# A fused attention and gated-MLP kernel: the second batch's first head pair goes through the opening, transposed by TensorE

## The chip, the cores and the metric

The kernel runs on one core of a Trainium2 chip. A core has five engines that run side by side, each with its own stream of instructions: TensorE (PE in the profile; its weight loads are listed apart as PEld), VectorE (DVE), ScalarE (ACT), GpSimd (POOL) and SyncE (SP), which here only issues DMA transfers. They meet at semaphores. PE writes into PSUM, which has eight banks here: four singles (the tags m0 to m3) and two doubles (s0, s1). Everything else lies in SBUF, 128 partitions wide.

The metric is the device time of one execution in microseconds (us); lower is better.

## The reference, cut to what matters

```
# q, k, v: (8 batches, 8 heads, 576 positions, 64)
scores = q @ k.T / 8
scores = where(block_i >= block_j, scores, -1e9)    # blocks of 64 positions
attn = exp(scores - max); attn = attn / (sum(attn) + 1e-9)
x = (attn @ v), heads side by side                  # (8, 576, 512)
h = relu(x @ w_in)                                  # 1024 wide
u, v = h[..., :512], h[..., 512:]
v_n = (v - mean(v)) / sqrt(var(v) + 1e-6)
v_s = w_spatial @ v_n + b_spatial                   # over the 576 positions
out = (u * v_s) @ w_out
```

## The kernel before

Work is counted in **pairs** of heads (four to a batch, 32 in all) and in **batches** of the MLP (eight). The batches' MLP matmuls are "M" work; they use a split of each number in a high and a low part and three products in place of one. A batch of M consists of five groups of v (L1103; the fifth is short, for the last 64 positions), eight groups of u (L1213), eight spatial groups (L1250 to L1257) and eight output groups (L1302). `moe(b, ready)` lists them; the string `order` says in which order the groups of v and u come. All groups of v of a batch need x, the attention's result, of all four pairs of that batch.

There are two forms of attention.

- **The opening** (function `opening`) does the four pairs of batch 0, cut into 16 units (k, pair): `unit(k, pr)` takes query rows in four parts k = 0 to 3. For each unit: scores on PE (L897, L907), row maxima on DVE with a mask added (L935, L941), exponentials on ACT (L951), sums on POOL and their reciprocal on DVE, a scaling on POOL or ACT (L370, L372), then PE transposes the scaled scores in blocks of 128 x 128 (L993) into PSUM, ACT or DVE copies them into the tile pt (L366), and PE multiplies them with v (L1021). The result is split into x by ACT (L1036) and DVE (L1040). Scaled scores of all units lie in the two buffers of the tile p, at places that `place(k, pr)` gives; a place is used again when the transposes that read it are through. Parts of pt serve in turn, three of them.
- **All later pairs** (function `attention`) do their scores in one row of instructions (L587, L603), the softmax on the same engines (L657, L663, L685, L698, L704, L372), and then DVE transposes blocks of 32 x 32 inside each partition group (L726) and 16 transfers of SyncE's queue regroup the blocks from p into pt (L734). There is one tile pt, and a pair's regroup waits until the products of the pair before it (L750) are through. There are two buffers of p. For the keys to come out in the right order, the host permutes k for these pairs. Batch 1 (`plain`) takes q and k as they are, later batches split them into a high and a low part (`need`).

**The order of all instructions is fixed ahead**, by the class `Line`: every piece of work is added with its engine, an assumed duration, what it comes after, which buffers it takes and drops (`Hold`, `Ring`, `Banks`) and a rank; `play` then goes through time and gives each engine the ready piece of the lowest rank. PE has four lanes, in each of which the order is kept: S (scores), T (transposes), A (products), M (the MLP). `pick_pe` takes A, T or S ahead of M when they are ready; a piece's `slack` is added to the time at which it counts as ready; a `gate` holds a score or a product back until a given amount of M work has been spent (`LEAD`, `MATE`, `MATE_LEAD`). Where the plan has a long wait on PE, `bridge` fills it with `pad` matmuls (L346, L350), which compute nothing. SyncE's queue is ordered by rank in the same way: loads of raw q and k, of v and of weights, the regroup, and the stores of the output.

**Weights** are prepared in the same stretch: w_in (L426 to L446, L393, L396), in two halves (for v and for u), w_spatial and w_out, each loaded into one of two staging tiles, converted on DVE, ACT and POOL and split. The last argument of `prep_w_in`, `prep_w_sp`, `prep_w_tail` and `prep_w_out` is the rank.

**Tiles that serve twice**: the mask of the opening (`mask0`) lies in the tile vl3, which the first MLP batch needs later; v_n waits for it by `mask_hold`. `tails[b]` (tag xs, two buffers) holds the last 64 positions of x of a batch.

Of the kernel before, what the change touches and what calls it, by code (L numbers as in the profile page):

```python
# [17 lines left out]
P = 128  # L18
S = 576
# [238 lines left out]
def kernel(  # L258
# [41 lines left out]
    mask0 = ff_p.tile([P, S], F32, tag="vl3", name="mask0")  # L300
# [60 lines left out]
    mask_hold = given(r_vn, 9 * NPAIR + 14)  # L361
# [39 lines left out]
    def prep_w(hi, lo, w, rows, cols, name, rank):  # L401
# [10 lines left out]
        f_hold = mask_hold if home else Hold(r_vr, 2)  # L412
# [102 lines left out]
    def attention(b, pr):  # L515
# [213 lines left out]
        for j in range(4):  # L729
            for i in range(4):  # L730
                def regroup(i=i, j=j):
                    if "pt" not in box:
                        box["pt"] = pt_p.tile([P, 4, NT, 32], F32, tag="pt", name=f"pt_{nm}")
                    nc.sync.dma_start(  # L734
                        box["pt"][32 * j:32 * j + 32, i], box["pp"][32 * i:32 * i + 32, j]
                    )
# [39 lines left out]
        al.slack = 100 if plain else None  # L776
# [34 lines left out]
    def opening():  # L811

        boxes = [{} for _ in range(NPAIR)]
# [26 lines left out]

        def load_part(pr, n):
            spans = (slice(0, 256), slice(Q0, Q0 + 256)), (slice(256, Q0), slice(Q0 + 256, KQ))
            for m, cs in enumerate(spans[n]):
                def fn(cs=cs, start=n == m == 0):
                    if start:
                        boxes[pr]["raw"] = raw_tile(pr)
                    nc.sync.dma_start(boxes[pr]["raw"][:, cs], qk[0, pr, :, cs])
# [3 lines left out]
                    "SP", 340, fn, takes=takes,  # L851
                    rank=-4 + 0.01 * len(got), size=P * 4 * (cs.stop - cs.start)))

        def load_v(pr):
            def fn():
                if pr < 2:
# [5 lines left out]
                nc.sync.dma_start(t, v[0, pr])  # L862
# [12 lines left out]
        load_v(3)  # L875

        def unit(k, pr):
            nm = f"0_{pr}_{k}"
# [49 lines left out]
            for r, (hd, o, n, at) in enumerate(runs):  # L928
# [36 lines left out]
            a = add("POOL", 190, guard, after=sums, rank=-1)  # L965
            a = add("DVE", 165, lambda: nc.vector.reciprocal(box["sum"][:, 4:4 + n], box["sum"][:, 0:n]),
                    after=[a], rank=-1.5)
            muls = [[], []]
            for r, (hd, _, cols, _) in enumerate(runs):
# [3 lines left out]
                m = add(("POOL", "ACT"), (240 + 0.825 * cols, 120 + 0.845 * cols), scale, after=[a], rank=0)  # L973
# [5 lines left out]
            for z, (t0, m) in enumerate(split):  # L979
# [15 lines left out]
                def move(eng, z=z, t0=t0, m=m):  # L995
# [8 lines left out]
                                 after=[a], drops=[t_hold], rank=-0.5))  # L1004
# [26 lines left out]
            def high():  # L1031
                if k == 0:
                    xts[0, pr] = xt_p.tile([P, 2, S], F32R, tag="x", name=f"x_0_{pr}")
                    if pr == 0:
                        tails[0] = ff_p.tile([P, NPAIR, 2, 64], F32R, tag="xs", name="xs_0", bufs=2)
                nc.scalar.copy(xts[0, pr][:, 0, q0:q0 + n_q], box["av"][:, 0, :n_q])  # L1036
# [7 lines left out]

            takes = [x_hold[0, pr]] + ([xs_hold[0]] if pr == 0 else []) if k == 0 else []
            h = add("ACT", 60 + 0.82 * n_q, high, after=[a], takes=takes, drops=[a_hold], rank=-3,
                    behind=x_done.get((0, pr), [])[:1])
            x_done.setdefault((0, pr), []).append(
                add("DVE", 70 + 1.045 * n_q, low, after=[h], drops=[a_hold], rank=-3))
            if k == 3:  # L1050
                def tail():
                    nc.gpsimd.tensor_scalar(
                        out=tails[0][:, pr], in0=xts[0, pr][:, :, FULL * P:].bitcast(F32), scalar1=1.0,
# [3 lines left out]
                xs_done[0, pr] = add("POOL", 271, tail, after=x_done[0, pr], rank=-1)  # L1057

        for k in range(4):
            for pr in range(NPAIR):  # L1060
                unit(k, pr)

    def x_need(b, first, last):

        edges = (256, 384, 512, 576) if b == 0 else (256, 576)
        return [
            x_done[b, pr][n] for pr in range(NPAIR) for n, (lo, hi) in enumerate(zip((0, *edges), edges))
# [5 lines left out]
    def moe(b, ready):  # L1073
# [164 lines left out]
        def sp_group(z, dc):  # L1238
# [35 lines left out]
            def rest():  # L1274
# [10 lines left out]
                    wide=True, rank=0.2 if last else 0.6)  # L1285
# [41 lines left out]
        order = "vuvuvuvuvuuuu" if b else "vvvvuuuuuvuuu"  # L1327
# [87 lines left out]
```

## Time and profile before

| | us |
|---|---|
| median of 3 runs | 673.7 (673.68 to 673.82) |
| the profiled execution | 671.56 |
| its span, first to last instruction | 669.8 |
| granted TensorE clock, mean | 1.00 |

A line of the timeline has the start, the length, the engine, the line of the kernel, the operation with what it writes and reads, the shape and the count; idle time ahead of it and what ended that stand in brackets. A matmul's length overlaps the next one's, so the price of one in a row is the distance between starts. SPq is SyncE's DMA queue. A line of the windows has a stretch and its length, then for PE, PEld, DVE, ACT and POOL the busy time and the number of instructions, then the granted clock, the mean share of the DMA engines and GB/s. A line of the groups has an engine, an operation, its count, the busy time, the mean ns of one, and the idle time before them with what ended most of it.

### The profile page before, as it was taken

The page shows a single profiled execution, that of the slowest core. Times are in us where ns is not written, and L with a number is a line of the kernel's source. Part 1 is how long each engine was busy: PE and PEld are TensorE (multiplying, and loading weights), DVE is VectorE, ACT ScalarE, POOL GpSimd, SP SyncE. Part 2 cuts the span into 40 slices and gives each one's busy share as a digit, 9 for nine tenths or more (in the row PEclk, how much of TensorE's full clock was granted, in tenths as well). Part 3 has the DMA queues.
Part 4 walks back from the last instruction along what each step waited for, and adds up shares of the span by engine and source line. Part 5 has one row for each costly group of instructions (what it writes and reads, how often), then busy time and mean ns, then how long its engine had stood idle before and what let it go on. Part 6 is the DMA issues. An engine that isn't in the chain of part 4 may idle for free.

```text
span 669.8 us, 15587 instructions
## 1 busy us (share of the span) xinstructions
PE 656.6 (98%) x5430; PEld 583.2 (87%) x5430; DVE 492.6 (74%) x1382; ACT 376.2 (56%) x1059; POOL 353.2 (53%) x688
## 2 busy tenths in 40 slices
PE   8999989989999999999999999999999999999998
PEld 5587978878999888998899888999889988999997
DVE  6989899766887669866898568877698668823522
ACT  7879777445755566545765645556665446512320
POOL 5377754365566635655656447665456556511111
PEclk9999999999999999999999999999999999999999
DMA  8164566664566664566456665585645664451002
GB/s 284 48 203 153 157 168 188 175 170 120 158 157 178 174 158 126 148 173 175 119 146 145 168 169 129 118 213 152 164 118 140 176 166 109 120 129 42 1 1 71
DMA packets 44210, 95.57 MB, mean 143 GB/s; under 512 B 9698, under 2 KB 19938, under 8 KB 44132
## 3 DMA queue, kind: packets, MB, share of 16 engines
q1 hardware_dynamic: 44132, 94.58, 52.6%
q8 instruction: 43, 0.70, 0.5%
q14 instruction: 35, 0.29, 0.1%
HBM read 39.23 MB, written 9.44 MB: 73 GB/s over the span
## 4 chain that ended last, share of the span: by engine, by line
PE 87%; SPq 5%; ACT 3%; DVE 2%; DMA 2%; issue 1%; POOL 1%; POOLq 0%; ACTq 0%
PE mo L1302 14%; PE mv L1103 14%; PE ms L1250 14%; PE mu L1213 12%; PE av L750 12%; PE s L587 8%; SPq L734 5%; PE s L603 3%; PE t L993 2%; PE av L1021 2%; ACT p L951 1%; PE ms L1255 1%; PE pad L350 1%; PE ms L1257 1%; PE s L907 1%
## 5 line engine op out<-in xcount | busy, mean ns | idle before, releaser
L372 POOL TENSOR_SCALAR p<-p,ssum 128x128 f32<-128x128 f32 (+5 forms) x261 | 152.2, 596 | 20.4 <-DVE ssum L704 8.8
L685 ACT ACTIVATE p<-p,nmax 128x128 f32<-128x128 f32 (+4 forms) x252 | 145.9, 581 | 26.1 <-DVE nmax L657 24.7
L726 DVE STREAM_TRANSPOSE p<-p 128x384 f32<-128x384 f32 (+2 forms) x196 | 121.3, 638 | 20.4 <-POOL p L372 19.2
L1213 PE MATMUL mu<-x,wi_hi 128*128 128x288 f32 x512 | 109.6, 295 | 0.0
L657 DVE CUSTOM_DVE_ANT_1 p<-s,mask 128x128 f32<-128x128 f32 (+1 forms) x224 | 95.3, 485 | 2.5 <-PE s L587 2.3
L750 PE MATMUL av<-pt,v 128*64 128x64 f32 (+2 forms) x1232 | 83.7, 291 | 6.7 <-DMA pt<-p 3.9
L750 PEld LDWEIGHTS av<-pt,v 128*64 128x64 f32 x1232 | 63.9, 137 | 28.5 <-issue 5.8
L1103 PE MATMUL mv<-wi_hi,x 128*128 128x512 f32 x256 | 87.1, 398 | 0.0
L1213 PEld LDWEIGHTS mu<-x,wi_hi 128*128 128x128 f32 x512 | 84.5, 188 | 1.8 <-DVE nmax L657 0.8
L1250 PE MATMUL ms<-ws_lo,vh 128*128 128x288 f32 x256 | 76.2, 298 | 0.0
L1250 PE MATMUL ms<-ws_hi,vh 128*128 128x288 f32 x256 | 75.8, 296 | 0.0
L1302 PE MATMUL mo<-gl,wo_hi 128*128 128x288 f32 x256 | 75.6, 295 | 0.0
L1250 PE MATMUL ms<-ws_hi,vl 128*128 128x288 f32 x256 | 75.6, 295 | 0.0
L1302 PE MATMUL mo<-gh,wo_lo 128*128 128x288 f32 x256 | 75.6, 295 | 0.0
L698 POOL TENSOR_SCALAR ssum<-ssum 128x4 f32<-128x4 f32 (+1 forms) x112 | 27.3, 243 | 91.2 <-ACT p L685 74.8
L1302 PE MATMUL mo<-gh,wo_hi 128*128 128x288 f32 x256 | 75.3, 294 | 0.0
L1213 PE MATMUL mu<-x,wi_lo 128*128 128x288 f32 x256 | 70.7, 297 | 0.0
L1272 ACT CAST gh<-u 128x288 fp32r<-128x288 f32 x64 | 25.9, 431 | 73.9 <-DVE u L1264 38.2
L790 DVE TENSOR_TENSOR x<-av,x 128x256 fp32r<-128x256 f32 (+1 forms) x56 | 25.4, 454 | 50.6 <-ACT x L787 50.2
L787 ACT CAST x<-av 128x256 fp32r<-128x256 f32 (+1 forms) x56 | 22.4, 399 | 69.2 <-PE av L750 69.1
L557 POOL TENSOR_TENSOR lo<-raw,hi 128x320 fp32r<-128x320 f32 (+1 forms) x72 | 57.7, 815 | 2.7 <-ACT hi L551 2.4
L1103 PEld LDWEIGHTS mv<-wi_hi,x 128*128 128x128 f32 x256 | 47.8, 188 | 12.6 <-issue 2.9
(130 smaller groups left out, 1541.9 us busy)
## 6 DMA issues: line engine op xcount, KB each, us to landing
pt<-p SPq DMA_DIRECT2D x448, 100.0 KB, 2.2
raw<-qk SPq DMA_DIRECT2D x28, 640.0 KB, 4.6
v<-v SPq DMA_DIRECT2D x32, 320.0 KB, 3.5
outT<-o SPq DMA_DIRECT2D x64, 144.0 KB, 2.0
rwi<-w_in SPq DMA_DIRECT2D x8, 512.0 KB, 4.6
rwo<-w_out SPq DMA_DIRECT2D x4, 512.0 KB, 3.9
raw<-qk SPq DMA_DIRECT2D x8, 192.0 KB, 4.7
rws<-w_spT SPq DMA_DIRECT2D x4, 288.0 KB, 3.2
```

The costliest lines, as they stand in the source:

```text
L372: nc.gpsimd.tensor_scalar(out=x, in0=x, scalar1=by, scalar2=1.0, op0=ALU.mult, op1=ALU.mult)
L557: eng.tensor_tensor(out=box["lo"][:, cs], in0=box["raw"][:, cs], in1=box["hi"][:, cs].bitcast(F32), op=ALU.subtract,)
L587: nc.tensor.matmul(by_block(bk[hd][:, o:o + n]), a[js, qs], keys(kk, js, n), start=(m == 0), stop=(m == len(parts) - 1),)
L657: nc.vector.tensor_tensor_reduce(out=out, in0=by_block(bk[hd][:, o:o + n]), in1=tiles(mask, 5 - t, t + 1), scale=-0.125, scalar=BIG, op0=A ...
L685: nc.scalar.activation(out, out, AF.Exp, bias=mx, scale=-1.0, accum_out=box["sum", k][:, c:c + 1],)
L726: nc.vector.transpose(x, x)
L734: nc.sync.dma_start(box["pt"][32 * j:32 * j + 32, i], box["pp"][32 * i:32 * i + 32, j])
L750: nc.tensor.matmul(box["av", z][js, q0:q1], box["v"][:, c, js], move(j), start=(n == 0), stop=(n == len(todo) - 1), skip_group_check=True,)
L1103: nc.tensor.matmul(box["ps"], a, w[:, k, DH:], start=(n == 0), stop=(n == len(todo) - 1))
L1213: nc.tensor.matmul(box["ps"][:, :HT], w[:, k, ds], xts[b, k][:, j, zs], start=(n == 0), stop=(n == len(todo) - 1),)
L1250: nc.tensor.matmul(box["ps"][:, :HT], vn[k][a][:, ds], w[:, k, zs], start=(n == 0), stop=False)
L1302: nc.tensor.matmul(box[ec, "ps"][:, :HT], w[:, k, es], a[:, k, :], start=(k == 0 and n == 0), stop=(last and n == 2),)
```

## The change

- Pair 0 of batch 1 (`MORE = 1`) leaves `attention` and becomes a fifth pair of `opening`: 4 more units, k = 0 to 3, put behind the 16 others, at four places of the second buffer of p. Its keys are not permuted by the host any more. Its ranks are by `LATER = 3` higher (less urgent) than those of batch 0. Its q and k come in four transfers into the tile raw when pair 0 of batch 0 is done with it.
- The mask's tile becomes a buffer of the tag xs, 512 wide, and is released after the row maxima of all 20 units; v_n waits for the weight preparation alone, and the second use of the other xs buffer (`tails[1]`, with the first x of the moved pair) waits for the mask.
- `LEAD` goes from 6.0 to 5.0: the gates of the pairs up to 9 (two pairs into batch 2) come a quarter batch of M work later.
- The regroup's rank goes from 2 to 1, the slack of batch 1's products from 100 to 1000 ns, the rank of w_in's u half from 0.7 to 0.65, of w_spatial from 1.45 to 0.8, of w_out from 2.6 to 1.1, and that of the gated low part on POOL from 0.6 to 0.3.
- The orders of the groups change: "vuvuvuvuvuuuu" becomes "vvuvuvuvuuuuu", and for batch 0 "vvvvuuuuuvuuu" becomes "vvvvuvuuuuuuu".

```diff
-LEAD = 6.0
+LEAD = 5.0
+MORE, LATER = 1, 3
...
-    mask0 = ff_p.tile([P, S], F32, tag="vl3", name="mask0")
+    mask0 = ff_p.tile([P, 512], F32, tag="xs", name="mask0", bufs=2)
...
-    mask_hold = given(r_vn, 9 * NPAIR + 14)
+    mask_hold, spare_hold = given(r_xs, 9 * (NPAIR + MORE)), given(r_vn, 14)
...
-                moved.append(add("SP", 635, regroup, after=done, drops=[pp_hold], rank=2, size=102400,
+                moved.append(add("SP", 635, regroup, after=done, drops=[pp_hold], rank=1, size=102400,
...
-        al.slack = 100 if plain else None
+        al.slack = 1000 if plain else None
...
-        boxes = [{} for _ in range(NPAIR)]
+        pairs = [(0, pr) for pr in range(NPAIR)] + [(1, pr) for pr in range(MORE)]
+        boxes = [{} for _ in pairs]
...
-        pp_holds = [Hold(r_pp, 7), Hold(r_pp, 9)]
+        pp_holds = [Hold(r_pp, 7), Hold(r_pp, 9 + 4 * MORE)]
...
+            if pr >= NPAIR:
+                return 1, (0, 3, 6, 10)[k], (3, 3, 4, 2)[k]
...
-        pt_hold = Hold(r_pt, 4 * NPAIR)
+        pt_hold = Hold(r_pt, 4 * len(pairs))
...
+        for pr in range(NPAIR, len(pairs)):
+            load_part(pr, 0)
+            load_part(pr, 1)
+            load_v(pr)
...
+            later = LATER if b else 0
...
-                a = add("DVE", 76 + 1.045 * n, rows, after=[op], drops=[s_hold[hd], mask_hold], rank=-2)
-                sums.append(add("ACT", 282 + 0.845 * n, exps, after=[a], rank=-1))
+                a = add("DVE", 76 + 1.045 * n, rows, after=[op], drops=[s_hold[hd], mask_hold], rank=later - 2)
+                sums.append(add("ACT", 282 + 0.845 * n, exps, after=[a], rank=later - 1))
...
+        for pr in range(NPAIR, len(pairs)):
+            for k in range(4):
+                unit(k, pr)
...
-                    wide=True, rank=0.2 if last else 0.6)
+                    wide=True, rank=0.2 if last else 0.3)
...
-        order = "vuvuvuvuvuuuu" if b else "vvvvuuuuuvuuu"
+        order = "vvuvuvuvuuuuu" if b else "vvvvuvuuuuuuu"
...
-    ready["u"] = [x for c in range(NC) for x in prep_w_in(c, 0, 0.7)]
-    ready["s"] = [x for c in range(FULL) for x in prep_w_sp(c, 1.45)] + prep_w_tail(1.45)
-    ready["o"] = [x for c in range(ND) for x in prep_w_out(c, 2.6)]
+    ready["u"] = [x for c in range(NC) for x in prep_w_in(c, 0, 0.65)]
+    ready["s"] = [x for c in range(FULL) for x in prep_w_sp(c, 0.8)] + prep_w_tail(0.8)
+    ready["o"] = [x for c in range(ND) for x in prep_w_out(c, 1.1)]
...
-        for pr in range(NPAIR):
+        for pr in range(MORE if b == 1 else 0, NPAIR):
             attention(b, pr)
...
+    qk[1, :MORE, :, :S], qk[1, :MORE, :, S:Q0] = kt[1, :MORE], 0
```

More of the change, by code (lines that the diff above doesn't have):

```diff
@@ L846, in fn @@
                         boxes[pr]["raw"] = raw_tile(pr)
-                    nc.sync.dma_start(boxes[pr]["raw"][:, cs], qk[0, pr, :, cs])
+                    nc.sync.dma_start(boxes[pr]["raw"][:, cs], qk[(*pairs[pr], slice(None), cs)])
                 takes = [raw_holds[pr]] if n == m == 0 else []
                 got.setdefault((pr, n), []).append(add(
-                    "SP", 340, fn, takes=takes,
+                    "SP", 340, fn, takes=takes, behind=() if takes else got[pr, 0][:1],
                     rank=-4 + 0.01 * len(got), size=P * 4 * (cs.stop - cs.start)))
@@ L855, in fn @@
             def fn():
-                if pr < 2:
+                if pr not in (2, 3):
                     t = v_p.tile([P, FULL + 1, P], F32, tag="v", name=f"v_0_{pr}")
@@ L963, in guard @@
                 )
-            a = add("POOL", 190, guard, after=sums, rank=-1)
+            a = add("POOL", 190, guard, after=sums, rank=later - 1)
             a = add("DVE", 165, lambda: nc.vector.reciprocal(box["sum"][:, 4:4 + n], box["sum"][:, 0:n]),
-                    after=[a], rank=-1.5)
+                    after=[a], rank=later - 1.5)
             muls = [[], []]
@@ L971, in scale @@
                     times(eng, box["run", r][0], box["sum"][:, 4 + r:5 + r])
-                m = add(("POOL", "ACT"), (240 + 0.825 * cols, 120 + 0.845 * cols), scale, after=[a], rank=0)
+                m = add(("POOL", "ACT"), (240 + 0.825 * cols, 120 + 0.845 * cols), scale, after=[a], rank=later)
                 muls[hd].append(m)
@@ L1003, in unit @@
                 moves.append(add(("ACT", "DVE"), (60 + 0.82 * P * m, 70 + 1.05 * P * m), move,
-                                 after=[a], drops=[t_hold], rank=-0.5))
+                                 after=[a], drops=[t_hold], rank=later - 0.5))
             q0, n_q = ((0, 256), (256, P), (384, P), (512, 64))[k]
@@ L1032, in high @@
                 if k == 0:
[L1033 to L1036, printed above, removed]
+                    xts[who] = xt_p.tile([P, 2, S], F32R, tag="x", name=f"x_{b}_{lane_pr}")
+                    if lane_pr == 0:
+                        tails[b] = ff_p.tile([P, NPAIR, 2, 64], F32R, tag="xs", name=f"xs_{b}", bufs=2)
+                nc.scalar.copy(xts[who][:, 0, q0:q0 + n_q], box["av"][:, 0, :n_q])
             def low():
-                x = xts[0, pr]
+                x = xts[who]
                 nc.vector.tensor_tensor(
@@ L1043, in low @@
                 )
[L1045 to L1049, printed above, removed]
+            takes = [x_hold[who]] + ([xs_hold[b]] if lane_pr == 0 else []) if k == 0 else []
+            h = add("ACT", 60 + 0.82 * n_q, high, after=[a], takes=takes, drops=[a_hold], rank=later - 3,
+                    behind=x_done.get(who, [])[:1])
+            x_done.setdefault(who, []).append(
+                add("DVE", 70 + 1.045 * n_q, low, after=[h], drops=[a_hold], rank=later - 3))
             if k == 3:
@@ L1052, in tail @@
                     nc.gpsimd.tensor_scalar(
-                        out=tails[0][:, pr], in0=xts[0, pr][:, :, FULL * P:].bitcast(F32), scalar1=1.0,
+                        out=tails[b][:, lane_pr], in0=xts[who][:, :, FULL * P:].bitcast(F32), scalar1=1.0,
                         scalar2=1.0, op0=ALU.mult, op1=ALU.mult,
                     )
-                xs_done[0, pr] = add("POOL", 271, tail, after=x_done[0, pr], rank=-1)
+                xs_done[who] = add("POOL", 271, tail, after=x_done[who], rank=later - 1)
         for k in range(4):
@@ L1061, in opening @@
                 unit(k, pr)
+        for pr in range(NPAIR, len(pairs)):
+            for k in range(4):
+                unit(k, pr)
     def x_need(b, first, last):
[L1065 removed]
+        edges = {4: (256, 384, 512, 576), 2: (256, 576)}
         return [
[L1067 removed]
+            done for pr in range(NPAIR) for x in [x_done[b, pr]]
+            for done, lo, hi in zip(x, (0, *edges[len(x)]), edges[len(x)])
             if lo < last and hi > first
```

13 lines of the change are left out of this document (7 added, 6 removed).

## The prediction, made before the changed kernel ran

> Pairs are called by batch and pair: 1.0 is the first pair of the second batch, the one that is moved. "Its products" are its score matrix times v (L750, and L1021 in the opening).
>
> **What bounds the kernel now.** The first look goes to the busy times and to the chain of work that ended last.
>
> ```profile
> span 669.8 us, 15587 instructions
> PE 656.6 (98%) x5430; PEld 583.2 (87%) x5430; DVE 492.6 (74%) x1382; ACT 376.2 (56%) x1059; POOL 353.2 (53%) x688
> PE 87%; SPq 5%; ACT 3%; DVE 2%; DMA 2%; issue 1%; POOL 1%; POOLq 0%; ACTq 0%
> ```
>
> TensorE (PE) is the bound of the whole; what can be won is 13.2 us of idle time (669.8 - 656.6) and whatever of the busy time is no work. The second look is at stretches cut at the places where pairs 1.0 to 1.3 get their products (columns: stretch, its length, busy time and count of PE, PEld, DVE, ACT, POOL, clock, DMA share, GB/s).
>
> ```profile
> 48.70:72.20 23.50, 23.50 (x148) 17.76 (x147) 22.60 (x74) 22.02 (x65) 17.68 (x32) 1.00 0.47 155
> 72.20:88.00 15.80, 13.31 (x95) 12.69 (x93) 13.30 (x26) 10.13 (x20) 9.03 (x12) 1.00 0.66 167
> 88.00:104.00 16.00, 14.68 (x130) 12.72 (x132) 15.80 (x44) 11.01 (x30) 7.72 (x15) 1.00 0.64 171
> 104.00:120.00 16.00, 15.01 (x129) 13.01 (x129) 14.53 (x44) 11.80 (x30) 6.55 (x13) 1.00 0.69 189
> 120.00:137.20 17.20, 15.53 (x145) 14.30 (x143) 10.76 (x33) 9.77 (x29) 9.25 (x16) 1.00 0.67 184
> 218.00:669.80 451.80, 448.46 (x3714) 407.69 (x3712) 311.78 (x855) 226.76 (x642) 227.85 (x451) 1.00 0.51 131
> ```
>
> From 218 us on PE is busy for 448.46 of 451.80 us; nothing that happens there can win much. Between 72 and 137 us it loses 6.5 us, and DVE is busy for 66.2 of the 71.3 us from 48.7 to 120. PE's own timeline says what it waits for there.
>
> ```profile
> 68.52 3.96 PE L350 MATMUL pad<-ident 128*128 128x128 f32 x34
> ...
> 88.09 2.96 PE L750 MATMUL av<-pt,v 128*64 128x256 f32 x44 [2.58 <-DVE u L1228]
> 90.98 2.43 PE L587 MATMUL s<-raw 64*128 64x128 f32 x16
> ...
> 96.12 3.06 PE L350 MATMUL pad<-ident 128*128 128x128 f32 x26
> ...
> 103.85 2.96 PE L750 MATMUL av<-pt,v 128*64 128x256 f32 x44 [1.23 <-DMA pt<-p]
> ...
> 119.82 2.96 PE L750 MATMUL av<-pt,v 128*64 128x256 f32 x44 [0.99 <-DMA pt<-p]
> ...
> 137.22 2.96 PE L750 MATMUL av<-pt,v 128*64 128x256 f32 x44 [1.70 <-DMA pt<-p]
> ```
>
> Four products wait 2.58 + 1.23 + 0.99 + 1.70 = 6.5 us. Two rows of pads, matmuls that compute nothing, are waits in disguise: 34 in 3.96 us is about 112 ns a pad, so 34 + 26 of them hold 6.7 us. The four products stand 15.8, 16.0 and 17.4 us apart. What sets this step is in SyncE's queue.
>
> ```profile
> 72.36 3.13 SPq L734 DMA_DIRECT2D pt<-p  x5
> ...
> 91.08 10.87 SPq L734 DMA_DIRECT2D pt<-p  x16
> ```
>
> ```profile
> pt<-p SPq DMA_DIRECT2D x448, 100.0 KB, 2.2
> ```
>
> One pair's regroup is 16 transfers; they take 10.9 us to issue, the last lands 2.2 us later, the products take 2.9, and only then is the single tile pt free for the next pair: 16.0 us. The second batch's matmuls with the weights (L1103, from 140.2 us, the end of pair 1.3's products) need all four pairs, so four turns of this chain stand one behind the other, from 72.4 to 140.2 us. In that stretch the chain is the bound, DVE is close behind, and PE third.
>
> **The change part by part.** It takes one of the four turns out of the chain: 1.0 goes through the opening, where PE transposes and a copy from PSUM writes pt. Each term:
>
> What it removes: 16 of 64 transfers ahead of 140 us, 7 DVE transposes, and one products group on PE.
>
> ```profile
> L726 DVE STREAM_TRANSPOSE p<-p 128x384 f32<-128x384 f32 (+2 forms) x196 | 121.3, 638 | 20.4 <-POOL p L372 19.2
> ```
>
> What it adds is priced by the same work of pairs 0.0 to 0.3 in the opening; a price is the distance from one start to the next.
>
> ```profile
> 18.41 0.92 PE L907 MATMUL s<-raw 64*128 64x384 f32 x4
> 19.25 0.87 PE L1021 MATMUL av<-pt,v 128*64 128x256 f32 x8
> 20.06 0.55 PE L993 MATMUL t<-ident,p 128*128 128x128 f32 x3
> ...
> 27.07 3.81 PE L907 MATMUL s<-raw 64*128 64x512 f32 x12
> ...
> 36.24 1.97 PE L993 MATMUL t<-ident,p 128*128 128x128 f32 x16
> 38.14 1.97 PE L1021 MATMUL av<-pt,v 128*64 128x128 f32 x32
> ...
> 46.78 1.24 PE L897 MATMUL s<-raw 128*128 128x288 f32 x4
> 47.94 0.80 PE L1021 MATMUL av<-pt,v 128*64 128x64 f32 x20
> 48.67 0.50 PE L1103 MATMUL mv<-wi_hi,x 128*128 128x512 f32 x1
> ...
> 50.27 2.43 PE L587 MATMUL s<-raw 64*128 64x128 f32 x16
> 52.62 0.66 PE L993 MATMUL t<-ident,p 128*128 128x128 f32 x4
> ...
> 62.41 1.24 PE L603 MATMUL s<-raw 128*128 128x320 f32 x4
> 63.24 0.64 PE L1103 MATMUL mv<-wi_hi,x 128*128 128x512 f32 x1
> 63.72 0.40 PE L1103 MATMUL mv<-wi_lo,x 128*128 128x512 f32 x1
> 63.95 0.40 PE L1103 MATMUL mv<-wi_hi,x 128*128 128x512 f32 x1
> ```
>
> Pair 1.0 on PE today: scores 2.35 for k = 0 to 2 and, by the row of pair 1.1, 0.83 for k = 3; products 2.89 (88.09 to 90.98), together 6.1 us. In the opening's form: scores 0.84 for k = 1, the same taken for k = 0, 3.81 / 3 = 1.27 for k = 2, 1.16 for k = 3, sum 4.1; transposes 6 + 6 + 8 + 5 = 25 at 1.90 / 16 = 119 ns, 3.0; products 0.81 for k = 0, the same for k = 1, 1.97 / 2 = 0.98 for k = 2 and 0.73 for k = 3, sum 3.3. Together 10.4: **4.3 us more PE work**. It is also cut into more pieces that break a run of weight matmuls: 4 scores for 2, 4 products for 1, and 8 groups of transposes, 13 more breaks. One break costs 0.48 - 0.23 = 0.25 us (the first mv behind the score against the next). Between nothing, if all stand side by side, and 13 x 0.25 = 3.3 us I take 1.5, six breaks, since transposes and products of one pair often adjoin in the rows above. PE work grows by 5.8 us, between 4.3 and 7.6.
>
> A page of the Trainium skill speaks against this: "TensorE: Matmul & The Clock Gate", Part 4, says that a transpose takes about 275 ns in a kernel and does not count as activity that lifts the clock. The trace does not bear it out: 16 of them start 119 ns apart, and the stretches above have clock 1.00 (25 at the page's figure would be 6.9 us for 3.0, an estimate by that page).
>
> What goes: with 1.0 out of the chain the 2.58 us wait ahead of its products goes, and the pads at 68.5 us, since its transposes and products come due in just that stretch and fill it. The pads at 96 us wait for the spatial matmuls' last operand, made from the short fifth group of v; the new order "vvvvuv..." puts that group after one u for five. The three waits on pt (3.9 us together) go if the chain comes early enough. Now each bound on the start of the second batch's weight matmuls, 140.2 us today:
>
> - PE: 140.2 - 6.5 - 6.7 + 5.8 = **132.8 us**.
> - DVE: it loses 7 x 0.638 = 4.5 us and gains between 0 and 4.2 (25 blocks of 128 columns, by the row below; ACT may take them instead), 2.1 taken. If it never idles from 48.7 us, its 66.2 us end at 48.7 + 66.2 - 2.4 = 112.5; regroup and products of 1.3 add 10.9 + 2.2 + 2.9: 128.5 us.
> - The chain: 1.0's first score can't start before the last transposes of pair 0.3 leave its place in p (52.62). Today 1.0 takes from 50.27 (score) to 72.36 (all transposed) 22 us; so it is through at about 75, with copies and products 80. Then 1.1's regroup: 80 + 10.9 + 2.2 = 93, 1.2's products at 109, 1.3's at 125, their end 128 us.
>
> ```profile
> L366 DVE COPY pt<-t x4: 292/680/691, 40.7 to 53.6; 128x512 f32<-128x512 f32 x3, 128x128 f32<-128x128 f32 x1
> ```
>
> So PE itself becomes the bound, with 4 us of slack to the others. An order fixed ahead doesn't use slack fully; I let one of the three waits on pt stay (3.9 / 3 = 1.3 us): 134.1, a gain of **6.1 us**.
>
> The rest I cost at nothing, each between -1.2 and +1.2 us, the size of a wait on pt above: the mask tile (the same additions, another place); the loads of 1.0, issued as four transfers in place of one from when raw falls free, cover being DVE's backlog; LEAD 5, which holds the scores of 1.2, 1.3 and of batch 2 back by a quarter batch of weight matmuls, but score 2.0 stands at about that place already, as its buffer in p is freed by 1.2's regroup; the slack of 1000 ns, which puts matmuls in front of products whose transfers may be late, hidden as long as weight matmuls are there; ranks of weight preparation and of the regroup, which shuffle work within a full DVE and SyncE (where w_out's preparation displaces a softmax, the chain's 4 us of slack cover it); orders "vvu...", where PE hasn't idled.
>
> Against the profiled execution's 671.56 us (span 669.8 and 1.8 around it) that makes 665.5. The median of the three runs is 673.7, 2.1 above it; the gain is taken off that: **667.6 us**.
>
> **The rivals.**
>
> (a) *More goes than I count.* Later the chain of batch 2 makes PE wait once more:
>
> ```profile
> 200.47 2.90 PE av L750 x44
> ...
> 215.91 2.46 PE pad L350 x22
> 218.36 2.90 PE av L750 x44
> ```
>
> If that pad goes too, no wait stays and no break costs: -13.2 - 2.5 + 4.3 = -11.4, 662.3 us. For it: the chain is early by a turn. Against: scores 2.0 and 2.1 are tied to a place in the weight matmuls. Chance 0.10.
>
> (b) *DVE and ACT stay the bound*, as 22.60 and 22.02 of 23.50 us say, and 1.0's small pieces queue there: 1.0 is through at 87, not 80, the chain ends at 135 and with the same left-over waits at 137: -3, 670.7 us. Chance 0.16.
>
> (c) *Given back later.* Batch 2's products stand 17.9 us apart (200.47 to 218.36), which is near the chain's least (2.9 + 11 + 2.2, and other transfers between). If this chain starts no earlier, the pads at 216 grow by what was won: 673.7 us. Against: score 2.0 waits for 1.2's regroup, which moves. Chance 0.08.
>
> (d) *Slower: 1.0 holds pt too long.* 1.1's regroup now waits for the last of four product groups, which need one of two double PSUM banks that scores also take, and whose first copy into x waits until the mask's tile is free, that is for all rows of 1.0. The point is 91 us, where 1.1's regroup starts today: from there each us late is a us lost, since PE then has no other work. At 95 us the time is 677.7. For it: DVE full, the new pieces ranked behind the weights. Against: today's 22 us. Chance 0.13.
>
> (e) *A transpose on PE costs its whole length.* The profile gives 285 ns as its mean; 25 x 285 = 7.1 us for 3.0: 671.7 us. The distance of 119 ns above speaks against it. Chance 0.03. (The rule of the Trainium skill's page "TensorE: Matmul & The Clock Gate" would have it so.)
>
> ```profile
> L993 PE MATMUL t<-ident,p 128*128 128x128 f32 x100 | 15.5, 285 | 0.9 <-POOL p L372 0.5
> ```
>
> **How the numbers follow.** The forecast has 0.50, its own range 664.5 to 670 (7.6 us of added work and two waits more, to all waits gone). The range of 8 in 10 takes in (a), (b), (c) and (e) and leaves out (d): 662.2 to 673.9. A measurement of this kernel can tell about 0.2% (1.35 us) from no change. Faster by more: 0.50 + 0.10 + 0.14 of (b) + 0.02 of (e) = 0.76; within: 0.02 + 0.07 + 0.01 = 0.10; slower: 0.13 + 0.01 of (c) = 0.14.
>
> **What would show it.** Right: 432 transfers at L734 for 448, 189 stream transposes, 125 PE transposes; no wait near 88 us; no pads at 68 or 96; products of 1.1 at about 93, and the first weight matmul of batch 1 near 134 us. (b) shows as 1.1's products near 100; (c) as pads ahead of 2.3's products; (d) as 1.1's regroup starting after 91; (e) as transposes 285 ns apart. The forecast is wrong if PE has idle time or pads of more than 6 us between 48 and 140.

## The result, and the profile after

| | before | after |
|---|---|---|
| median of the runs, us | 673.76 (673.68 to 675.11, 4 runs) | 664.62 (664.26 to 667.92, 4 runs) |
| the profiled execution, its span | 671.56, 669.8 | 664.53, 662.8 |
| end of batch 0's output groups, us | 152.6 | 149.6 |
| of batch 1's | 233.5 | 226.9 |
| of batch 7's | 666.7 | 659.4 |

The changed kernel takes 0.9871 of the time of the kernel before, 95% interval 0.9837 to 0.9904. The forecast was 667.6 us, 6.1 us of gain; the medians differ by 9.1, the two profiled executions by 7.0. The ends in the table are those of the last output matmul of a batch in PE's timeline. By them batch 0 wins 3.0 us, batch 1 another 3.6, and the six others together 0.7.

The page of the changed kernel, its busy times, the chain of work that ended last by engine, and the group of stream transposes:

```profile
span 662.8 us, 15520 instructions
...
PE 654.2 (99%) x5403; PEld 580.3 (88%) x5403; DVE 490.0 (74%) x1377; ACT 378.4 (57%) x1068; POOL 348.9 (53%) x689
...
PE 90%; DVE 5%; POOL 2%; ACT 1%; issue 1%; SPq 0%; DMA 0%; POOLq 0%; DVEq 0%
...
L727 DVE STREAM_TRANSPOSE p<-p 128x384 f32<-128x384 f32 (+2 forms) x189 | 117.4, 640 | 13.8 <-POOL p L373 11.3
```

SyncE's queue has left the chain (5% before, 0% now) and PE's share rose from 87 to 90%. The counts are those of the edit: 189 stream transposes. The DMA issues of the changed kernel say the same of the regroup:

```profile
pt<-p SPq DMA_DIRECT2D x432, 100.0 KB, 2.2
```

PE's timeline of the changed kernel, in lines numbered 1 to 14 higher than before (L993 is L1003, L1021 is L1031, L1103 is L1117, L1213 is L1227, L750 is L751):

```profile
40.69 1.97 PE L1003 MATMUL t<-ident,p 128*128 128x128 f32 x16
42.58 1.97 PE L1031 MATMUL av<-pt,v 128*64 128x128 f32 x32
...
71.21 0.39 PE L1117 MATMUL mv<-wi_hi,xs 128*128 128x512 f32 x1
...
72.32 0.52 PE L1003 MATMUL t<-ident,p 128*128 128x128 f32 x3 [0.25 <-DVE u L1242]
...
80.17 2.02 PE L1031 MATMUL av<-pt,v 128*64 128x128 f32 x36
82.12 0.40 PE L1227 MATMUL mu<-x,wi_hi 128*128 128x288 f32 x1
...
95.41 1.95 PE L351 MATMUL pad<-ident 128*128 128x128 f32 x16
97.97 2.97 PE L751 MATMUL av<-pt,v 128*64 128x256 f32 x44 [0.61 <-DVE st L1150]
100.86 2.43 PE L588 MATMUL s<-raw 64*128 64x128 f32 x16
103.12 1.05 PE L347 MATMUL pad<-ident 64*128 64x128 f32 x8
...
113.50 2.96 PE L751 MATMUL av<-pt,v 128*64 128x256 f32 x44 [0.77 <-DVE p L727]
...
129.56 2.96 PE L751 MATMUL av<-pt,v 128*64 128x256 f32 x44 [0.22 <-issue]
```

Three products of L751 stand where four stood, and their waits are 0.61 + 0.77 + 0.22 us; with 0.25 at 72.3 that is 1.85 in place of 6.5. The 34 pads at 68 and the wait of 2.58 us at 88 are gone. Of the 26 pads at 96, 16 stay, and 8 stand at 103: 24 at 112 ns are 2.7 us in place of 6.7. So waits and pads fell from 13.2 to 4.6 us, by 8.6. The moved pair's last products end at 82.1 us. SyncE's queue takes up the regroup 2.8 us after that:

```profile
84.90 11.21 SPq L735 DMA_DIRECT2D pt<-p  x16
...
101.01 10.84 SPq L735 DMA_DIRECT2D pt<-p  x16
...
116.54 10.94 SPq L735 DMA_DIRECT2D pt<-p  x16
```

It starts at 84.9; before, the same pair's transfers started at 91.1. What PE does with the time is read from its busy time in stretches, first of the changed kernel, then of the one before, cut close to the first matmul with the weights of batch 0 and of batch 1:

```profile
0.00:49.30 49.30, 46.36 (x397) 32.39 (x397) 39.67 (x136) 39.08 (x115) 25.43 (x56) 1.00 0.54 170
49.30:137.40 88.10, 86.21 (x689) 72.15 (x686) 76.60 (x220) 69.52 (x187) 55.21 (x96) 1.00 0.59 169
```

```profile
0.00:48.70 48.70, 45.38 (x398) 31.71 (x398) 39.80 (x136) 39.09 (x115) 25.52 (x56) 1.00 0.52 173
48.70:140.20 91.50, 85.00 (x686) 73.08 (x684) 78.36 (x221) 65.39 (x175) 53.06 (x90) 1.00 0.62 176
```

Without the pads PE's work up to that matmul was 45.4 + 85.0 - 6.7 = 123.7 us and is now 46.4 + 86.2 - 2.7 = 129.9: 6.2 us more. The balance: 8.6 us of waits and pads and 0.4 us of idle time in the opening go, 6.2 us of work come, and the cut moves by 2.8 us, from 140.2 to 137.4. The chain of work says what sets this start:

```profile
135.50 1.59 PE ms L1264 x12
...
137.36 2.75 PE mv L1117 x12
```

Batch 1's weight matmuls (mv) now follow spatial matmuls of batch 0 without a wait, while the last products of its attention ended at 132.5. Before, they followed those products directly. PE, not the regroup, is the bound there now. Batch 1's 3.6 us: its 22 pads (2.46 us at 216) are gone, and six more with them that PE's timeline of the kernel before has:

```profile
181.32 0.83 PE L350 MATMUL pad<-ident 128*128 128x128 f32 x6
```

The next matmul starts at 182.08, so these six hold 0.76 us. The other 0.4 aren't assigned to rows.

### The profile page after: what moved, and what is told of

It reads as the page before. It is cut to its first block, busy times and chain, and to the rows that moved or that the text cites. A ratio compares the mean times of both kernels' runs of the same rounds, so it can differ in the third digit from the quotient of the medians.

```text
span 662.8 us, 15520 instructions
## 1 busy us (share of the span) xinstructions
PE 654.2 (99%) x5403; PEld 580.3 (88%) x5403; DVE 490.0 (74%) x1377; ACT 378.4 (57%) x1068; POOL 348.9 (53%) x689
## 4 chain that ended last, share of the span: by engine, by line
PE 90%; DVE 5%; POOL 2%; ACT 1%; issue 1%; SPq 0%; DMA 0%; POOLq 0%; DVEq 0%
PE mo L1316 15%; PE mv L1117 14%; PE ms L1264 14%; PE mu L1227 14%; PE av L751 12%; PE s L588 8%; PE s L604 3%; PE t L1003 2%; PE av L1031 2%; PE s L917 2%; PE ms L1269 1%; PE ms L1271 1%; POOL p L373 1%; DVE p L658 1%; DVE p L951 1%
## 5 line engine op out<-in xcount | busy, mean ns | idle before, releaser
L373 POOL TENSOR_SCALAR p<-p,ssum 128x128 f32<-128x128 f32 (+5 forms) x262 | 150.1, 588 | 22.8 <-DMA pt<-p 8.2
L686 ACT ACTIVATE p<-p,nmax 128x128 f32<-128x128 f32 (+4 forms) x243 | 140.7, 581 | 19.1 <-DVE nmax L658 17.4
L727 DVE STREAM_TRANSPOSE p<-p 128x384 f32<-128x384 f32 (+2 forms) x189 | 117.4, 640 | 13.8 <-POOL p L373 11.3
L1227 PE MATMUL mu<-x,wi_hi 128*128 128x288 f32 x512 | 110.4, 298 | 0.0
L658 DVE CUSTOM_DVE_ANT_1 p<-s,mask 128x128 f32<-128x128 f32 (+1 forms) x216 | 92.2, 486 | 0.7 <-PE s L588 0.7
L1227 PEld LDWEIGHTS mu<-x,wi_hi 128*128 128x128 f32 x512 | 84.1, 188 | 6.7 <-issue 4.8
L1117 PE MATMUL mv<-wi_hi,x 128*128 128x512 f32 x256 | 85.3, 395 | 0.0
L751 PE MATMUL av<-pt,v 128*64 128x64 f32 (+2 forms) x1188 | 80.1, 290 | 1.9 <-DVE p L727 0.8
L751 PEld LDWEIGHTS av<-pt,v 128*64 128x64 f32 x1188 | 61.7, 137 | 21.1 <-issue 3.3
L699 POOL TENSOR_SCALAR ssum<-ssum 128x4 f32<-128x4 f32 (+1 forms) x108 | 25.0, 231 | 86.4 <-ACT p L686 81.4
L1227 PE MATMUL mu<-x,wi_lo 128*128 128x288 f32 x256 | 70.1, 295 | 0.0
L1289 POOL TENSOR_TENSOR gl<-u,gh 128x288 fp32r<-128x288 f32 x48 | 38.8, 823 | 43.2 <-ACT gh L1286 43.1
L1117 PEld LDWEIGHTS mv<-wi_hi,x 128*128 128x128 f32 x256 | 48.0, 188 | 10.4 <-issue 0.8
L1117 PE MATMUL mv<-wi_lo,x 128*128 128x512 f32 x128 | 50.5, 394 | 0.0
```

The source lines that it names most:

```text
L373: nc.gpsimd.tensor_scalar(out=x, in0=x, scalar1=by, scalar2=1.0, op0=ALU.mult, op1=ALU.mult)
L658: nc.vector.tensor_tensor_reduce(out=out, in0=by_block(bk[hd][:, o:o + n]), in1=tiles(mask, 5 - t, t + 1), scale=-0.125, scalar=BIG, op0=A ...
L686: nc.scalar.activation(out, out, AF.Exp, bias=mx, scale=-1.0, accum_out=box["sum", k][:, c:c + 1],)
L727: nc.vector.transpose(x, x)
L751: nc.tensor.matmul(box["av", z][js, q0:q1], box["v"][:, c, js], move(j), start=(n == 0), stop=(n == len(todo) - 1), skip_group_check=True,)
L1117: nc.tensor.matmul(box["ps"], a, w[:, k, DH:], start=(n == 0), stop=(n == len(todo) - 1))
```

## The experiments

The change has three main parts that can be undone one by one: the fifth pair, the orders of the v and u groups, and the urgencies (ranks and slack). Four theories were held against each other. **A**: the turn taken out of the chain is the gain, the rest only keeps up with it; this is the prediction's. **B**: the orders and urgencies are the gain. **C**: PE's added work eats the turn, so that it pays only where the orders have work ready. **D**: it is the urgency of the weights. C and D were put down after e1 to e3. Ratios are to runs of the kernel before on the same chip. The last column takes only runs whose mean granted clock over the span is recorded as 1.000 (their number, of how many); its use comes below. Brackets hold the 95% interval.

| kernel | pair | orders | urgencies | median, us | ratio | at clock 1.000, us |
|---|---|---|---|---|---|---|
| before | | | | | 1 | 671.9 (5 of 46) |
| e2 | x | | | 674.06 | 0.9999 [0.9982, 1.0015] | 673.6 (5 of 10) |
| e10 | | x | | 672.49 | 0.9972 [0.9953, 0.9991] | 670.4 (1 of 10) |
| e12 | | | x | 671.42 | 0.9955 [0.9938, 0.9972] | 671.4 (4 of 6) |
| e5 | x | x | | 673.09 | 0.9980 [0.9963, 0.9998] | 672.4 (2 of 10) |
| e3 | x | | x | 671.35 | 0.9951 [0.9934, 0.9968] | 671.4 (4 of 6) |
| e1 | | x | x | 670.89 | 0.9943 [0.9921, 0.9966] | 670.3 (3 of 4) |
| after | x | x | x | 664.62 | 0.9871 [0.9837, 0.9904] | 664.5 (3 of 4) |

`LEAD` is 6.0 in the kernel before, e2, e10 and e12 and 5.0 in the others. The mask has its new place in all but the kernel before, e10 and e12; that was not undone by itself. The last column has no intervals: its runs of one kernel lie up to 3.0 us apart (e2, 671.9 to 674.9), so it can't tell differences of about 1 us.

### One part undone, or one part alone

**e1**, the change without the fifth pair:

```diff
-MORE, LATER = 1, 3
+MORE, LATER = 0, 3
```

> The changed kernel with MORE = 0: pair 1.0 goes back to attention and its regroup; the new ranks, orders, LEAD, slack and the mask's tile stay. Theory A (the gain comes from taking one of four turns out of the chain of regroups): four turns of 16 us stand ahead of the second batch's weight matmuls again, the wait near 88 us and most of the waits on pt are back; at most the pads at 96 us stay away; 670 to 674 us. Theory B (the gain comes from orders and urgencies, which bring weight matmuls and the short group of v in time): 666 to 669 us, with four product groups 16 us apart all the same but fewer idle microseconds and pads between 48 and 140 us than the 13.2 of before.

**e2**, the fifth pair and the mask's new place alone; the rest as before (the edit is against the changed kernel):

```diff
-LEAD = 5.0
+LEAD = 6.0
-                moved.append(add("SP", 635, regroup, after=done, drops=[pp_hold], rank=1, size=102400,
+                moved.append(add("SP", 635, regroup, after=done, drops=[pp_hold], rank=2, size=102400,
-        al.slack = 1000 if plain else None
+        al.slack = 100 if plain else None
-                    wide=True, rank=0.2 if last else 0.3)
+                    wide=True, rank=0.2 if last else 0.6)
-        order = "vvuvuvuvuuuuu" if b else "vvvvuvuuuuuuu"
+        order = "vuvuvuvuvuuuu" if b else "vvvvuuuuuvuuu"
...
+    ready["u"] = [x for c in range(NC) for x in prep_w_in(c, 0, 0.7)]
+    ready["s"] = [x for c in range(FULL) for x in prep_w_sp(c, 1.45)] + prep_w_tail(1.45)
+    ready["o"] = [x for c in range(ND) for x in prep_w_out(c, 2.6)]
```

> The kernel before with pair 1.0 in the opening and the mask in the other tile, but with the old ranks, slack, LEAD and orders. Theory A: the chain is one turn shorter, so the waits on pt go, the pads near 96 us (the short fifth group of v is still late) stay: 666 to 669 us. Theory B: 672 to 676 us, since 5 to 6 us of PE work are added and the weight matmuls still don't come in time, which shows as more pads or idle time between 48 and 140 us.

**e3**, the change with both old orders:

```diff
-        order = "vvuvuvuvuuuuu" if b else "vvvvuvuuuuuuu"
+        order = "vuvuvuvuvuuuu" if b else "vvvvuuuuuvuuu"
```

> The changed kernel with the two old order strings alone. Theory A: the short group of v is late again and costs about the 2.9 us of pads that stood at 96 us before: 666 to 669 us. Theory B: 670 us or more; the pads and waits of before come back although the chain has three turns.

The three came out at 0.9943, 0.9999 and 0.9951. By the times that were expected, e2 (674.06 us) and e3 (671.35) fit theory B, and e1 (670.89) fits theory A, so neither holds for all three. Theory A fell with e2: the fifth pair alone is worth nothing, and at like clock it costs 1.7 us. It does what it should to the chain. PE's timeline of e2:

```profile
95.04 1.95 PE L351 MATMUL pad<-ident 128*128 128x128 f32 x16
99.36 2.97 PE L751 MATMUL av<-pt,v 128*64 128x256 f32 x44 [2.37 <-DMA pt<-p]
...
115.78 2.97 PE L751 MATMUL av<-pt,v 128*64 128x256 f32 x44 [0.93 <-DVE p L727]
...
122.91 1.28 PE L351 MATMUL pad<-ident 128*128 128x128 f32 x10
...
132.23 2.96 PE L751 MATMUL av<-pt,v 128*64 128x256 f32 x44 [1.10 <-DVE nmax L658]
...
218.06 2.62 PE L351 MATMUL pad<-ident 128*128 128x128 f32 x22
```

The last products start at 132.2 in place of 137.2 us, 5 us sooner. Waits of 2.37 + 0.93 + 1.10 = 4.4 us and 16 + 10 = 26 pads (2.9 us) remain, with smaller waits elsewhere 8.0 us against 13.2. But batch 0 ends at 153.6 us, 1.0 later than before, so that 5.2 + 1.0 = 6.2 us of PE work have come in, as many as after the change; the pads at 218 stand as they did at 216. So one turn less and its price on PE cancel, which is one half of theory C.

In e1 the chain has its four turns again. PE's timeline of e1:

```profile
68.58 3.96 PE L351 MATMUL pad<-ident 128*128 128x128 f32 x34
...
89.69 3.97 PE L751 MATMUL av<-pt,v 128*64 128x256 f32 x36 [0.57 <-DVE u L1242]
...
98.46 3.51 PE L351 MATMUL pad<-ident 128*128 128x128 f32 x30
```

The pads at 68 that the fifth pair fills after the change are back, and 30 more at 98; another 26 stand at 136.7. These 90 pads hold 10.1 us, and 4.6 us of waits come to them, which is no less than the 13.2 us before, where theory B expected less. (That 36 products take 3.97 us is told at the end.) Theory B alone gives less than half of the gain. From e1 to the changed kernel the fifth pair is worth 0.9943 - 0.9871 = 0.7%, with intervals that don't meet; alone it was worth nothing.

**e5**, the pair and the new orders with the old ranks and slack, **e10**, the new orders alone in the kernel before, and **e12**, the ranks and slack alone in the kernel before:

```diff
(e5, against the changed kernel)
-rank=1, ... al.slack = 1000 ... wide=True, rank=0.2 if last else 0.3 ... 0.65, 0.8, 0.8, 1.1
+rank=2, ... al.slack = 100 ... wide=True, rank=0.2 if last else 0.6 ... 0.7, 1.45, 1.45, 2.6
(e10, against the kernel before)
-        order = "vuvuvuvuvuuuu" if b else "vvvvuuuuuvuuu"
+        order = "vvuvuvuvuuuuu" if b else "vvvvuvuuuuuuu"
(e12, against the kernel before)
-rank=2, ... al.slack = 100 ... wide=True, rank=0.2 if last else 0.6 ... 0.7, 1.45, 1.45, 2.6
+rank=1, ... al.slack = 1000 ... wide=True, rank=0.2 if last else 0.3 ... 0.65, 0.8, 0.8, 1.1
```

> The changed kernel with the old ranks and the old slack (fifth pair, new orders and LEAD stay). Theory C (the fifth pair's added PE work eats what its turn in the chain gives, and the gain comes only where the freed time is filled: by orders that have weight matmuls ready): the orders do most of it, so close to the changed kernel, 665 to 668 us. Theory D (the ranks do it: w_spatial and w_out prepared early are what gives PE matmuls at 95 to 125 us): 670 us or more, with pads there.

> The kernel before with the two new order strings alone. Theory C: the pads near 96 us go or shrink, and each later batch is the 0.15 us shorter that the changed kernel shows (77.3 for 77.45 us), but the four turns of regroups still bound the first batch: 670 to 673 us. If orders worked by themselves it would be 668 us or less; by theory D 673 to 674 us.

> The kernel before with the new ranks and the slack of 1000 ns alone. Theory C: nothing to -2 us (the chain bounds), 671.5 to 674 us. Theory D: 670 us or less.

They came out at 0.9980, 0.9972 and 0.9955. The three single parts sum to 0.01 + 0.28 + 0.45 = 0.74%, all three together win 1.29%. Any two of them win no more than 0.57%. At like clock the single parts are worth -1.7, 1.5 (one run) and 0.5 us, 0.3 together, and all three 7.4; taken out of the changed kernel, the pair costs 5.8 us (e1), the orders 6.9 (e3) and the urgencies 7.9 (e5). So no part carries the gain; it is there when all three are. That is more than theory C said, which expected e5 at 665 to 668 us; and e12 is not the 670 us or less of theory D. e5 shows a part of why the pair and the orders alone don't do it. PE's timeline of e5:

```profile
99.93 4.63 PE L751 MATMUL av<-pt,v 128*64 128x256 f32 x44 [3.07 <-DMA pt<-p]
```

The products wait 3.07 us for the regroup (the next two 1.24 and 1.52 us), and then take 4.63 us for 2.97 (more on this at the end).

### Which item of the orders and urgencies

**e4**, the change with the old `LEAD`; **e6**, with the old order of batch 0 alone; **e13**, with the old slack alone; **e14**, with the old ranks of the weights alone:

```diff
(e4)
-LEAD = 5.0
+LEAD = 6.0
(e6)
-        order = "vvuvuvuvuuuuu" if b else "vvvvuvuuuuuuu"
+        order = "vvuvuvuvuuuuu" if b else "vvvvuuuuuvuuu"
(e13)
-        al.slack = 1000 if plain else None
+        al.slack = 100 if plain else None
(e14)
-prep_w_in(c, 0, 0.65) ... prep_w_sp(c, 0.8) ... prep_w_tail(0.8) ... prep_w_out(c, 1.1)
+prep_w_in(c, 0, 0.7) ... prep_w_sp(c, 1.45) ... prep_w_tail(1.45) ... prep_w_out(c, 2.6)
```

> The changed kernel with LEAD 6.0. All theories: no difference to the changed kernel, 664 to 666 us, since scores 1.2 to 2.1 wait for their buffer of p and not for the gate. If the gate of 5.0 does bind, the batch 2 chain starts earlier and the time changes by over 1 us.

> The changed kernel with batch 0's old order (the short group of v after five groups of u in place of one); the later batches keep the new one. If the short group's lateness is what the old orders cost, its pads near 95 to 108 us are back (70 of them, 7.8 us, in the kernel with both old orders): 668 to 671 us. If the later batches' order does it: 664 to 667 us.

> The changed kernel with the old slack of 100 ns alone. If the waits of 5.8 us on pt in the kernel with old ranks came from PE taking the products too early, they come back here at 97, 113 and 130 us (some 3 to 5 us together): 667 to 670 us. If they came from the late weights or from SyncE's order, the time stays at 664 to 666 us.

> The changed kernel with the old ranks of the weights alone (w_in's u half, w_spatial, w_out); slack and regroup rank stay new. If the weights' ranks carry the gain: 669 to 673 us, with pads ahead of spatial or output groups. If the slack and the regroup carry it: 664 to 667 us.

| kernel | median, us | ratio | at clock 1.000, us | profiled: end of batch 0, of batch 1, us |
|---|---|---|---|---|
| after | 664.62 | 0.9871 [0.9837, 0.9904] | 664.5 | 149.6, 226.9 |
| e4, old `LEAD` | 665.38 | 0.9863 [0.9836, 0.9891] | 665.4 (4 of 4) | not read |
| e6, old order of batch 0 | 670.32 | 0.9952 [0.9934, 0.9970] | 670.3 (7 of 7) | 153.2, 233.0 |
| e13, old slack | 668.75 | 0.9926 [0.9900, 0.9952] | 669.0 (2 of 4) | 154.0, 231.3 |
| e14, old ranks of weights | 666.90 | 0.9903 [0.9880, 0.9926] | 666.7 (2 of 4) | 150.8, 229.3 |

`LEAD` does nothing that shows. The ranks of the regroup and of POOL's low part were not undone by themselves. **Batch 0's order** is as large an item as any of these: e6 is within 0.1% of e3, so the orders of the later batches are worth little (from the end of batch 1 to that of batch 7, e3 takes 433.1 us and e6 432.1), and this one 5 to 6 us. PE's timeline of e6:

```profile
87.22 0.50 PE L1117 MATMUL mv<-wi_hi,xs 128*128 128x512 f32 x1
...
95.04 3.73 PE L351 MATMUL pad<-ident 128*128 128x128 f32 x32
...
99.62 2.97 PE L751 MATMUL av<-pt,v 128*64 128x256 f32 x44 [0.84 <-DMA pt<-p]
...
104.78 1.50 PE L347 MATMUL pad<-ident 64*128 64x128 f32 x12
...
107.38 2.84 PE L351 MATMUL pad<-ident 128*128 128x128 f32 x24
```

Here 32 + 12 + 24 = 68 pads stand where the changed kernel has 24. In the old order the short group of v waits until five groups of u are through, its matmuls (x of the last 64 positions) run at 87 us and not at 71, and the spatial matmuls that need it come later. That the changed kernel keeps 24 pads has a cause of its own. ACT's timeline of the changed kernel shows the copy of that short group out of PSUM:

```profile
93.88 0.59 ACT L1131 COPY vr<-mv 64x512 f32<-64x512 f32 x1 [0.41 <-DVE vl L1209]
```

Its matmuls were through at 74 us; the copy runs at 93.9, behind work of DVE on the group before, and the spatial matmuls behind it are what the pads at 95 and 103 stand in for. No run tried to bring it forward. In e6, where the group's matmuls run 16 us later, this copy is only 1.9 us later, at 95.8; the operand made from it (L1193) is written at 109.8 and not at 105.6. Why so little of the 16 us arrives was not traced.

**The slack**: PE's timeline of e13.

```profile
95.45 0.83 PE L351 MATMUL pad<-ident 128*128 128x128 f32 x6
98.15 2.97 PE L751 MATMUL av<-pt,v 128*64 128x256 f32 x44 [1.87 <-DMA pt<-p]
103.31 1.27 PE L347 MATMUL pad<-ident 64*128 64x128 f32 x10
105.69 2.84 PE L351 MATMUL pad<-ident 128*128 128x128 f32 x24
114.65 2.97 PE L751 MATMUL av<-pt,v 128*64 128x256 f32 x44 [1.73 <-DMA pt<-p]
130.55 3.31 PE L751 MATMUL av<-pt,v 128*64 128x256 f32 x44 [0.66 <-DVE nmax L658]
```

With a slack of 100 ns the fixed order puts the products where the plan has the transfers land; on the chip they land later, and the first two products wait 1.87 and 1.73 us for them. The third wait, 0.66 us, ends with row maxima on DVE, after the transfers have landed at 128.7 (the chain of work of e13). Behind the second and the third stand matmuls of groups already under way. Behind the first stand pads: the spatial matmuls begin at 108.3 and not at 105.0, as DVE scales the short group (L1177) at 105.7 and not at 100.5. So the slack also moves DVE's work in the fixed order, and the two effects weren't separated. With 0.24 at 72.4 and 40 pads (4.5 us) waits and pads are 9.0 us against 4.6 after the change, 4.4 more, and batch 0 ends 4.4 us later. A slack of 1000 ns puts the groups under way in front instead. The intervals of e13 and of the changed kernel just meet (0.9900 and 0.9904).

**The ranks of the weights**: 2.2 us at like clock, though the intervals of e14 and the changed kernel overlap. The chain of work of e14 goes through a late weight:

```profile
112.82 3.81 DMA rwo<-w_out
```

With rank 2.6 this piece of w_out lands at 116.6 us. PE's timeline of e14 has pads behind it:

```profile
120.28 2.17 PE L351 MATMUL pad<-ident 128*128 128x128 f32 x18
```

That the output groups wait for this piece there is read from the chain, not tried by itself. It explains little: up to the end of batch 0 the 18 pads (2.0 us) and PE's idle time (3.0 us) are 5.0 us together, against 4.6 after the change. Batch 0 ends 1.2 us later and batch 1 2.4; most of that isn't assigned to rows. The 666.90 us lie where they were expected if the slack and the regroup, and not the weights, carry the gain. So theory D, the weights alone, is not borne out.

### One step further

**e8** takes pair 1.1 into the opening as well, with the mask back in the tile vl3, and **e15** changes only how much less urgent the moved pair is:

```diff
(e8)
-MORE, LATER = 1, 3
+MORE, LATER = 2, 3
-    mask0 = ff_p.tile([P, 512], F32, tag="xs", name="mask0", bufs=2)
+    mask0 = ff_p.tile([P, S], F32, tag="vl3", name="mask0")
-    mask_hold, spare_hold = given(r_xs, 9 * (NPAIR + MORE)), given(r_vn, 14)
+    mask_hold = spare_hold = given(r_vn, 9 * (NPAIR + MORE) + 14)
...
(e15)
-MORE, LATER = 1, 3
+MORE, LATER = 1, 4
```

> Two pairs of the second batch through the opening (MORE = 2; the sixth raw tile is the one that pair 0.2 leaves, the mask is in vl3 again because two pairs would otherwise block each other's PSUM banks). If PE is the bound now, a second pair adds some 5 us of PE work and can take away no more than the 4.5 us of waits and pads that the changed kernel has left between 48 and 140 us: 664.5 to 669 us. If the chain of regroups still bounds, one more turn less gives a gain again: 660 to 663 us.

> The changed kernel with the moved pair one rank less urgent (LATER = 4), an attempt to beat it: the short group of v and the spatial operands come before the moved pair's copies on DVE and ACT, so the 4.5 us of waits and pads left between 48 and 140 us may shrink; but the regroup of 1.1 starts later than 85 us. 662.5 to 666.5 us if the first prevails; over 667 us if the chain does.

e8 took 667.62 us, 0.9898 [0.9879, 0.9917], and e15 664.27, 0.9864 [0.9840, 0.9888]. e8 has no pad at all between 48 and 140 us and 3.3 us of idle time, less than the 4.6 of waits and pads after the change, and is 3 us slower: that agrees with PE as the bound, where a second pair adds work with little left for it to fill. The windows of e8 up to its first weight matmul of batch 1 show the size:

```profile
0.00:49.30 49.30, 46.47 (x397) 32.52 (x397) 39.73 (x136) 39.07 (x115) 25.45 (x56) 1.00 0.54 170
49.30:140.60 91.30, 87.77 (x702) 71.33 (x699) 76.36 (x221) 68.44 (x185) 58.22 (x98) 1.00 0.49 145
```

The second window has no pads: 46.5 + 87.8 = 134.2 us of work stand against 129.9 after the change, about 4.4 us more, and the start of batch 1's weight matmuls moves from 137.4 to 140.6. e15 can't be told from the changed kernel; no version was found that beats both.

## Why the prediction was right, and where its working was not

The time fell inside the forecast's own range of 664.5 to 670 us, 3.0 us below the forecast and 0.1 above the lower end. By its steps:

- **One turn out of the chain; PE becomes the bound**: right. The start of batch 1's weight matmuls now follows PE's own work, but at 137.4 and not at 134.1 us: of the 6.1 us that were to be won there, 2.8 came. The chain's dates were 2 to 5 us too early throughout: 1.0 through at 82.1 and not 80, products at 98.0, 113.5 and 129.6 and not at 93, 109 and 125. It still ended ahead of PE.
- **PE's work**: 6.2 us more, against 5.8 (4.3 to 7.6). The transposes run 16 in 1.9 us, 118 ns apart (L1003, 40.69 to 42.58), so rival (e) fell.
- **What goes**: 13.2 - 1.3 = 11.9 us were expected to go from waits and pads, 8.6 went. The pads at 68 and the wait at 88 went as said; the pads at 96 shrank, with the short group's copy at 93.9 as the next thing late.
- **Batch 2's pads**: rival (a)'s row, the pads at 216, went against the forecast, and batch 1 won 3.6 us in all. The forecast counted nothing there.
- **"The rest I cost at nothing, each between -1.2 and +1.2 us"**: this is the step that failed. Undone by itself at like clock, the slack costs 4.5 us (669.0 - 664.5) and the ranks of the weights 2.2. `LEAD` (0.9 by e4) and the later orders (about 1.0, e3 against e6) stayed inside the 1.2. Batch 0's order, credited with the pads at 96 (2.9 us), is worth 5.8.
- **So the cause was mis-assigned**: the working gave the gain to the turn that was removed. e2 shows that turn alone to be worth nothing, its waits being paid back as PE work. Taken out of the changed kernel it costs 5.8 us at like clock, but the orders (6.9) and the urgencies (7.9) cost no less. By these runs PE wins only if, in the place of the waits, work is ready and is put ahead. That the total came out near is partly luck: the sum counted 3.3 us of waits and pads as gone that stayed, and left out 4.3 us that came behind the start of batch 1's weight matmuls (3.6 in batch 1, 0.7 after it).
- **"The gain is taken off" the median**: 2.1 us lay between the median and the profiled execution before; after, the profiled execution (664.53) is at the median. So the medians show 2.1 us more gain than the profiles. In the 46 runs of the kernel before beside the experiments, those with a mean clock of 1.000 took 671.6 to 672.7 us (5), with 0.997 673.0 to 674.8 (25), with 0.994 or 0.995 674.8 to 676.7 (16). Three of four runs after the change have 1.000; why the fourth, with 0.999, took 667.92 is open. In the kept traces with 0.999 (e2, e12) the clock drops only behind the last matmul. That the removed waits are what steadied the clock is argued from the next section's rows, not shown by a run of its own. e12 has the same pattern: 671.0 to 671.7 with clocks of 0.999 and 1.000, so its ratio of 0.9955 is mostly steadier clock, and only 0.5 us at like clock.

(d) didn't come: the regroup started at 84.9, ahead of the 91 from which it decides. Of (b) the sign came, 1.1's products at 98.0, nearer to its 100 than to 93, but not the price, since PE and not the chain set the start. (c) didn't come: no pads stand ahead of 2.3's products.

## What to carry to other kernels

When a wait is removed by moving its work to the engine that waits, the two prices can cancel; look for the ready work that is to fill the hole, and make it early before counting the hole as won. In an order that is fixed ahead, a planned landing time that is too early by a microsecond or two can make the engine wait in front of ready work, so a margin in the plan is an edit with a price, not a detail. Undo each part by itself and each alone: here three parts won 0.74% one by one and 1.29% together, at like clock 0.3 and 7.4 us.

## What the runs showed of the hardware

A wait of PE that no pads fill can cost more than its length. Windows of e5 around the end of its 3.07 us wait, of e10 around the end of one of 2.23 us, and of e1 around the end of two of 1.11 and 0.57 us:

```profile
96.70:100.11 3.41, 0.34 (x4) 0.21 (x4) 3.23 (x6) 0.99 (x2) 0.14 (x1) 1.00 0.71 177
100.11:103.52 3.41, 3.41 (x26) 2.69 (x25) 1.74 (x4) 1.68 (x3) 0.00 (x0) 0.50 0.25 97
```

```profile
134.41:137.82 3.41, 1.19 (x9) 0.96 (x9) 1.22 (x5) 2.21 (x6) 3.15 (x7) 1.00 0.81 166
137.83:141.24 3.41, 3.40 (x24) 2.43 (x26) 1.42 (x4) 1.10 (x2) 2.84 (x6) 0.50 0.79 303
```

```profile
86.48:89.89 3.41, 1.73 (x15) 1.19 (x16) 2.70 (x4) 2.13 (x5) 1.56 (x2) 1.00 0.77 205
89.89:93.30 3.41, 3.41 (x30) 2.38 (x28) 2.77 (x7) 0.68 (x1) 0.00 (x0) 0.50 0.42 139
```

Each time the granted clock falls to 0.50 for 3.41 us. In e5 and e10 the same 44 products took 4.63 and 4.61 us for 2.97: 1.65 us more. An estimate from this: one drop in 672 us makes a mean clock of 0.997 and costs 1.7 us, two make 0.995 and cost 3.4. That fits the groups of runs above, with medians of 671.9, 673.7 and 675.7. It isn't the length of the wait alone: behind the 2.37 us of e2 and the 2.58 us of the kernel before the products took 2.97 and 2.96.

Drops begin on a grid: in the clock records of e5, e10 and e1 it begins 28, 39 and 25 times 3.413 us after the clock's rise at the start. In the 3.41 us ahead of the drop PE was busy for 0.34, 1.19 and 1.73 us. The 2.58 us of the kernel before lie across a border of its grid at 86.20, with 1.52 us busy in the step behind it and no drop, so the busy time of a step doesn't settle it either. The Trainium skill, "TensorE: Matmul & The Clock Gate", Part 1, has the clock halved after at least one idle window of about 3.4 us, and the window free-running, not reset when a kernel starts. The grid and the length of the drops agree with that; that 1.73 us of work in the 3.41 us ahead did not prevent a drop does not agree with a whole idle window. Rows of pads up to 34 long were not followed by such a loss in the stretches read here.
